# Channel mixer in two groups of six blocks, and plain fp32 scores, in an attention and mixer kernel on one core

## The chip, the cores and the metric

The program runs on one core of one Trainium2 chip, in one launch. The metric is device time in microseconds (us), the median of three runs. A core has a matrix engine (PE, with its weight loads shown as PEld), a vector engine (DVE), an activation engine (ACT), a general engine (POOL), and queues that start DMAs; here all DMAs start from SP's queue (SPq).

## The reference

Four batches of 576 rows. Per batch: eight heads of attention that keep the 32 largest scores of each row, then a gated mixer, then a token mixer and a channel mixer.

```
scores = q @ k.T / 8;  keep the 32 largest of each row;  attn = softmax;  x = attn @ v     # 8 heads of 64
gate = sigmoid(5-tap causal convolution of x);   x = (gate * (x @ w_val)) @ w_out          # 512 x 512 weights
u = x + token mixer(x)                                                                      # 576 -> 256 -> 576
out = u + relu(u @ w_ch1) @ w_ch2                                                           # 512 -> 1536 -> 512
```

The last line is the channel mixer; its 1536 middle features are 12 blocks of 128 rows.

## The kernel before, in words

**Tiling.** Heads are taken in pairs: 16 pairs `p`, batch b = p // 4. A pair has five units: four of 128 query rows for both heads (tile 0 and 1 of a unit, L314 on), one with the last 64 rows of both. For each unit `attn` makes the scores in PSUM in two halves of 288 keys (`Sp`; in batch 0 also the two `mo` tiles), copies them to `S` (L339), folds and finds the 32 largest on DVE (L431, L444 to L446, L461, L463), masks (L374 on ACT, L376 on POOL), takes the exponential (L379), transposes on PE (L388) and multiplies by v (L401 to L405).

**Scores.** The constant `SPLIT = 1, 2, 3` names the batches whose scores are made from two rounded parts. For these `load_pair` splits the loaded `qk` into `qkh` and `qkl` (one ACT copy, L480, and one POOL subtraction, L481, for q and for k of each pair), and a half is six matmuls (`qk3`, L324): high by high, low by high, high by low, each for two heads that stand in rows 0 to 63 and 64 to 127 of the array. In batch 0 a half is two matmuls on the unsplit fp32 data (`qk`, L330), which the trace shows as four, two passes for each head. The last unit of a pair uses plain data in every batch (L348, L350).

**Mixers.** All other large products go through `mm3` (L543 to L545): for each term three matmuls on split operands, 288 columns each. The channel mixer in `mix` runs `G = 3` groups. A group makes four blocks of middle features (weights `ch1`; each block is 2 halves x 4 terms x 3 = 24 matmuls into one `mo` tile), rounds each into a high part (ACT, L487) and a low part (in batches 1 to 3 DVE, L496) in `rh[0..3]`, `rl[0..3]`, then four output tiles (weights `ch2`, 24 matmuls each), each added on to `f` by DVE (`plus`, L652). There are two `mo` tiles.

**Weights.** A weight piece is a `ring` slot (four slots of 128 x 2 x 512). The first time, in batch 0, `piece` loads the 64-bit source, turns it to fp32 on DVE (L515, L519), splits it (ACT, POOL) and stores it in device memory (`ch1d`, `ch2d`); the later batches load it back (L554).

**What sets the order.** `Order` collects all operations with a cost, their dependences and a priority, runs a list schedule for several rounds, and issues the operations in the order of the planned starts. Each engine then works its own queue in that order. So an edit can change the place of any instruction of any engine.

Of the kernel before, what the change touches and what calls it, by code (L numbers as in the profile page):

```python
# [15 lines left out]
NP = B * H // 2  # L16
NEG = -3.0e38
BIG = 2.0 ** 100
G = 3
LO = 1, 2, 3  # L20
CONV = 0,
XOFF = (7, 0, 0, 0)
ROUNDS = 4
PIECES = dict(val=4, out=4, ch1=12, ch2=12)
OFF = -2
WTOK = 24
SPLIT = 1, 2, 3
MOFF = (8, 0, -4, 0)
WOFF = 9

# [136 lines left out]
class Builder:  # L167
    def __init__(self, ctx, tc, qk, v, w_val, conv, w_out, w_tok1, w_tok2, w_ch1, w_ch2, out):
        self.tc, self.nc = tc, tc.nc
        self.qk, self.v, self.out, self.conv = qk, v, out, conv  # L170
        self.wsrc = dict(val=w_val, out=w_out, tok1=w_tok1, tok2=w_tok2, ch1=w_ch1, ch2=w_ch2)
        self.sb = ctx.enter_context(tc.tile_pool(name="sb", bufs=1))
        self.dr = ctx.enter_context(tc.tile_pool(name="dr", bufs=1, space=bass.MemoryType.DRAM))
        self.ps = ctx.enter_context(tc.tile_pool(name="ps", bufs=1, space=bass.MemoryType.PSUM))
        self.o = Order()
        T = self.T
        self.nS, self.nE, self.nW, self.nP = 4, 2, 2, 2
        self.stage = [T(f"stage{i}", [128, 1024], I32) for i in range(2)]
        self.vt = [T(f"v{i}", [128, 11, 64]) for i in range(2)]
        self.qk2 = [T(f"qk{i}", [128, 2, S]) for i in range(2)]  # L180
        self.qkp = [[T(f"qk{x}{i}", [128, 2, S], F32R) for x in "hl"] for i in range(2)]
        self.St = [T(f"S{i}", [128, 2, S]) for i in range(self.nS)]
        self.yt = T("y", [128, 2, S])
        self.At = T("A", [128, 2, 144])
        self.Xt = [T(f"X{i}", [128, 2, 168]) for i in range(2)]
        self.Zt = [T(f"Z{i}", [128, 2, 168]) for i in range(2)]
        self.top = [T(f"top{i}", [128, 2, 32]) for i in range(3)]
        self.nb = [T(f"nb{i}", [128, 2, 2]) for i in range(3)]
        self.Et = [T(f"E{i}", [128, 2 * S]) for i in range(self.nE)]
        self.Wt = [T(f"W{i}", [128, S]) for i in range(self.nW)]  # L190
        self.pT = [T(f"pT{i}", [128, 640]) for i in range(self.nP)]
        self.bad = T("bad", [128, NP * 5, 2, 3])
        self.cst, self.flag, self.worst = T("cst", [1, 1]), T("flag", [1, 1], I32), T("worst", [128, 1])
        self.den = [T(f"den{i}", [128, 4, 9]) for i in range(2)]
        self.rcp = T("rcp", [128, 4, 9])
        self.rhl = T("rhl", [128, 4, 64], F32R)
        self.rT = [T(f"rT{i}", [128, 128], F32R) for i in range(2)]
        self.sel = T("sel", [128, 768], F32R)
        self.ident = T("ident", [128, 128])
        self.diag = T("diag", [128, 5, 128])  # L200
        self.wv = {}
        for n, shp in (("tok1", [128, 2, 5, 256]), ("tok2", [128, 2, 2, S])):
            self.wv[n] = T("w" + n, shp, F32R)
        self.wa = [T(f"wa{i}", [128, S]) for i in range(2)]
        self.made = set()
        self.cw = T("cw", [128, 20])
        self.wd = {n: [self.dr.tile([128, 2, 512], F32, name=f"{n}d{i}") for i in range(k)]
                   for n, k in PIECES.items()}
        self.rs = [T(f"r{i}", [128, S], F32R) for i in range(16)]
        self.fs = [T(f"f{i}", [128, S]) for i in range(4)]  # L210
        self.tf = [T(f"t{i}", [128, S]) for i in range(2)]
        self.xf = [T(f"xf{i}", [128, 4 + S]) for i in range(4)]
        self.nring = 4
        self.ring = [T(f"ring{i}", [128, 2, 512]) for i in range(self.nring)]
        self.Sp = self.ps.tile([128, 2, 512], F32, name="Sp")
        self.PT = self.ps.tile([128, 1024], F32, name="PT")
        self.mo = [self.ps.tile([128, 2, 512], F32, name=f"mo{i}") for i in range(2)]
        self.cnt = dict(mo=0, tf=0, ring=0, rT=0, st=0, wa=0, unit=0, tile=0, load=0)
        self.slot = {}
# [64 lines left out]
    def load_pair(self, p):  # L284

        nc = self.nc
        b, c = divmod(p, 4)
        g = self.slot[p] = self.cnt["load"] % 2
        self.cnt["load"] += 1
        qk = self.qk2[g]  # L290
        for x in (1, 0):
            self.dma(2.3, lambda x=x: nc.sync.dma_start(qk[:, x], self.qk[b, c, :, x]), [], [("qk", g, x)])
        vt = self.vt[g]
        self.dma(2.5, lambda: nc.sync.dma_start(vt, self.v[p]), [], [("v", g)])
        if b in SPLIT and self.fast:
            hi, lo = self.qkp[g]
            for x in (1, 0):
                self.split(qk[:, x], hi[:, x], lo[:, x], [("qk", g, x)], [("qkh", g, x)], [("qkl", g, x)])

    def attn(self, p, u):  # L300

# [8 lines left out]
        R = [("qk", s, 0), ("qk", s, 1)]  # L310

        Sp, kSp = ((self.Sp, "Sp"), (self.mo[0], ("mo", 0)), (self.mo[1], ("mo", 1)))[i % 3 if b == 0 else 0]
        P = self.qkp[s]
        m, kM = self.top[i % 3], [("m", i % 3, t) for t in range(w)]  # L314
        if u < 4:

            for n in range(2):
                c0 = 288 * n

                def qk3(c0=c0):  # L320
                    for x, y in ((0, 0), (0, 1), (1, 0)):
                        for t in range(2):
                            r = slice(64 * t, 64 * t + 64)
                            nc.tensor.matmul(Sp[:, t, 0:288], P[x][r, 0, 128 * u:128 * u + 128],  # L324
                                             P[y][r, 1, c0:c0 + 288], start=(x + y == 0), stop=(x == 1))

                def qk(c0=c0):
                    for t in range(2):
                        r = slice(64 * t, 64 * t + 64)
                        nc.tensor.matmul(Sp[:, t, 0:288], q[r, 128 * u:128 * u + 128], k[r, c0:c0 + 288],  # L330
                                         start=True, stop=True)

                if b in SPLIT and self.fast:
                    self.pe(0.594, qk3, [(z, s, x) for z in ("qkh", "qkl") for x in range(2)], [kSp])
                else:
                    self.pe(0.686, qk, R, [kSp])
                if n and self.fast:
                    self.fold(i, w, St, (Sp[:, :, 0:288], Sp[:, :, 288:432]), kS, kSp)
                self.act(S, lambda c0=c0: nc.scalar.activation(St[:, :, c0:c0 + 288], Sp[:, :, 0:288], AF.Copy),  # L339
                         [kSp], [(x, n) for x in kS] + [kSp] * n)  # L340
# [207 lines left out]
    def piece(self, n, f):  # L548

        nc = self.nc  # L550
        w, k = self.nxt("ring", self.ring)
        kw = [(k, 0), (k, 1)]
        if (n, f) in self.made:
            self.dma(4, lambda: nc.sync.dma_start(w, self.wd[n][f]), [(n, f)], kw)  # L554
        else:
            self.made.add((n, f))
            prio = self.prio
# [1 line left out]
            d = self.dp, self.dd, self.da, self.dl  # L559
            self.dp = self.dd = self.da = self.dl = 0  # L560
            a, ka = self.nxt("wa", self.wa)
            self.f64(self.wsrc[n][f], a[:, 0:512], 128, ka)
            self.split(a[:, 0:512], w[:, 0].bitcast(F32R), w[:, 1].bitcast(F32R), [ka], kw[0:1], kw[1:])
            self.dma(4, lambda: nc.sync.dma_start(self.wd[n][f], w), kw, [(n, f)])
            self.prio = prio
            self.dp, self.dd, self.da, self.dl = d
        return w.bitcast(F32R).rearrange("p a (c f) -> p a c f", c=4), kw

    def gate(self, b, p0):
        nc = self.nc  # L570
# [83 lines left out]
    def mix(self, b):  # L654
# [42 lines left out]
        for c in range(4):  # L697
# [5 lines left out]
                                          for j in range(2)], km, 288)  # L703
            self.plus(x2[c], m, km, K("f", c))
            self.split(x2[c], uh[c], ul[c], K("f", c), K("r", c), K("r", c + 4))
        rh, rl = rs[8:12], rs[12:16]
        for g in range(G):
            for f in range(4):
                self.prio = p0 + 14 + 8 * g + f
                w, kw = self.piece("ch1", g * 4 + f)  # L710
                m, km = self.nxt("mo", self.mo)
                for n, s in halves():
                    self.mm3(m[:, n, 0:288], [(w[:, 0, kc], w[:, 1, kc], uh[kc][:, s], ul[kc][:, s],
                                               K("r", kc, kc + 4) + kw) for kc in range(4)], km, 288)
                self.parts(m[:, :, 0:288], S, two(rh[f]), two(rl[f]), True, b in LO,
                           [km], K("r", 8 + f), K("r", 12 + f))
            for c in range(4):
                self.prio = p0 + 16 + 8 * g + c
                w, kw = self.piece("ch2", g * 4 + c)
                m, km = self.nxt("mo", self.mo)  # L720
                for n, s in halves():
                    self.mm3(m[:, n, 0:288], [(w[:, 0, f], w[:, 1, f], rh[f][:, s], rl[f][:, s],
                                               K("r", 8 + f, 12 + f) + kw) for f in range(4)], km, 288)
                self.plus(fs[c], m, km, K("f", c))
                if g == G - 1:
                    self.dma(2.3, lambda c=c: nc.sync.dma_start(self.out[b, c], fs[c]), K("f", c), [("o", b, c)])
# [95 lines left out]
```

## Time and profile before

| | |
|---|---|
| median of 3 runs | 931.23 us (930.27 to 932.81) |
| profiled execution | 930.93 us, of which the span of instructions is 929.0 us |
| PE busy | 849.0 us (91%) |
| DVE busy | 763.4 us (82%) |
| ACT, POOL busy | 580.2 us (62%), 416.2 us (45%) |
| mean granted PE clock | 0.957 |

The span is what lies between the first and the last instruction; 1.9 us lie around it. A busy share of PE counts a pipelined matmul from its start to its modelled end, so what a matmul costs in a stream is read from the distance between starts. Attention ends at about 792 us; what follows is the last batch's gate, token mixer and channel mixer.

### The profile page before, as it was taken

The numbers are of one execution on the slowest core, as the hardware profiler recorded it, in microseconds if no ns is written. First come the engines' busy times: TensorE is split into PE (matmuls) and PEld (weight loads), VectorE is DVE, ScalarE is ACT, GpSimd is POOL, SyncE is SP. The second block draws the span as 40 slices with busy tenths as digits, with TensorE's granted clock in tenths as the row PEclk, the third lists the DMA queues.
The fourth block names the chain that finished last, engine by engine and source line by source line (L and its number), as shares of the span: only waits on it lengthen the run. The fifth ranks groups of instructions, "written<-read, shape, count | busy, mean of one in ns | idle before, by whom it ended". The sixth has DMA issues, their size and how long they took to land.

```text
span 929.0 us, 18621 instructions
## 1 busy us (share of the span) xinstructions
PE 849.0 (91%) x6649; PEld 731.1 (79%) x6649; DVE 763.4 (82%) x2653; ACT 580.2 (62%) x1279; POOL 416.2 (45%) x377
## 2 busy tenths in 40 slices
PE   4767758999999999999999999999999999889997
PEld 2444446798889987788888889888889999778997
DVE  8999999888999999996799999896997884812221
ACT  4767777857695867757677766676775754422000
POOL 2434555766785867653444433552542312502000
PEclk8878685999999999999999999999999999999999
DMA  3111022455145554623033334333033235222442
GB/s 117 38 47 39 30 67 90 176 180 186 41 162 199 184 186 158 219 92 117 17 121 106 114 108 152 123 117 108 29 105 114 92 106 195 92 92 75 169 164 103
DMA packets 33734, 107.48 MB, mean 116 GB/s; under 512 B 3872, under 2 KB 4128, under 8 KB 33632
## 3 DMA queue, kind: packets, MB, share of 16 engines
q1 hardware_dynamic: 33632, 106.20, 34.1%
q8 instruction: 54, 0.88, 0.4%
q14 instruction: 48, 0.39, 0.1%
HBM read 84.69 MB, written 21.50 MB: 114 GB/s over the span
## 4 chain that ended last, share of the span: by engine, by line
PE 57%; DVE 9%; ACT 6%; POOL 2%; issue 1%; DMA 1%; POOLq 0%; DVEq 0%; ACTq 0%; SPq 0%
PE mo L543 14%; PE mo L544 13%; PE mo L545 13%; PE PT L388 4%; PE Sp L324 4%; PE PT L401 4%; DVE f L630 2%; PE PT L405 2%; ACT r L487 1%; ACT E L379 1%; DVE top L461 1%; DVE Z L463 1%; PE Sp L348 1%; POOL E L376 1%; POOL r L481 1%
## 5 line engine op out<-in xcount | busy, mean ns | idle before, releaser
L543 PE MATMUL mo<-r,ring 128*128 128x288 f32 x1024 | 316.7, 309 | 2.1 <-DVE f L640 1.2
L544 PE MATMUL mo<-r,ring 128*128 128x288 f32 x1024 | 302.7, 296 | 3.0 <-POOL r L481 2.2
L545 PE MATMUL mo<-r,ring 128*128 128x288 f32 x1024 | 301.7, 295 | 0.2 <-POOL ring L481 0.2
L376 POOL TENSOR_TENSOR E<-S,W 128x576 f32<-128x576 f32 x144 | 209.9, 1474 | 89.0 <-ACT W L374 86.5
L543 PEld LDWEIGHTS mo<-r,ring 128*128 128x128 f32 x1024 | 192.3, 188 | 13.0 <-issue 7.8
L544 PEld LDWEIGHTS mo<-r,ring 128*128 128x128 f32 x1024 | 192.5, 188 | 5.3 <-POOL r L481 3.4
L545 PEld LDWEIGHTS mo<-r,ring 128*128 128x128 f32 x1024 | 192.2, 188 | 0.5 <-POOL ring L481 0.5
L388 PE MATMUL PT<-ident,E 128*128 128x128 f32 x656 | 106.7, 294 | 25.3 <-ACT E L379 13.5
L379 ACT ACTIVATE E<-E,nb 128x576 f32<-128x576 f32 x144 | 111.5, 775 | 25.4 <-POOL E L376 24.2
L461 DVE MAX8 top<-Z 128x8 f32<-128x168 f32 x432 | 126.1, 325 | 0.5
L393 ACT ACTIVATE pT<-PT 128x512 f32<-128x512 f32 (+1 forms) x144 | 94.3, 655 | 47.8 <-PE PT L388 47.2
L388 PEld LDWEIGHTS PT<-ident,E 128*128 128x128 f32 x656 | 79.4, 149 | 42.9 <-ACT pT L393 18.6
L374 ACT ACTIVATE W<-S,nb 128x576 f32<-128x576 f32 x144 | 106.1, 771 | 0.2
L487 ACT ACTIVATE r<-mo 128x576 fp32r<-128x576 f32 (+2 forms) x76 | 46.9, 632 | 85.8 <-PE mo L545 80.4
L401 PE MATMUL PT<-pT,v 128*64 128x128 f32 (+1 forms) x640 | 88.5, 286 | 12.0 <-ACT pT L393 11.3
L450 POOL TENSOR_TENSOR bad<-X,top 128x6 f32<-128x6 f32 (+1 forms) x80 | 23.1, 289 | 165.6 <-DVE top L461 153.7
L401 PEld LDWEIGHTS PT<-pT,v 128*64 128x64 f32 x640 | 69.4, 147 | 30.2 <-ACT pT L393 19.7
L652 DVE TENSOR_TENSOR f<-mo,f 128x576 f32<-128x576 f32 x64 | 48.0, 751 | 53.2 <-PE mo L545 53.0
L463 DVE MATCH_REPLACE8 Z<-top,Z 128x168 f32<-128x168 f32 x288 | 90.1, 319 | 0.0
L402 PE MATMUL PT<-pT,v 128*64 128x128 f32 (+1 forms) x640 | 88.5, 286 | 0.0
L339 ACT ACTIVATE S<-Sp 128x576 f32<-128x576 f32 x108 | 69.8, 647 | 26.6 <-DVE y L431 12.4
L481 POOL TENSOR_TENSOR r<-f,r 128x576 fp32r<-128x576 f32 x32 | 48.2, 1512 | 62.1 <-ACT r L480 62.0
(124 smaller groups left out, 1679.2 us busy)
## 6 DMA issues: line engine op xcount, KB each, us to landing
ring<-ch1d SPq DMA_DIRECT2D x36, 512.0 KB, 3.3
ring<-ch2d SPq DMA_DIRECT2D x36, 512.0 KB, 3.2
stage<-in_w_ch_dram SPq DMA_DIRECT2D x24, 512.0 KB, 3.6
qk<-in_qk_dram SPq DMA_DIRECT2D x32, 288.0 KB, 3.2
ch1d<-ring SPq DMA_DIRECT2D x12, 512.0 KB, 5.1
ch2d<-ring SPq DMA_DIRECT2D x12, 512.0 KB, 2.6
ring<-vald SPq DMA_DIRECT2D x12, 512.0 KB, 3.9
ring<-outd SPq DMA_DIRECT2D x12, 512.0 KB, 3.2
```

What stands on the lines that cost most here:

```text
L374: self.act(S, lambda W=W, x=x, t=t: nc.scalar.activation(W, x, AF.Relu, bias=nb[:, t, 1:2], scale=-BIG), kx + [(kN, 1)], [kW], True)
L376: self.pool(S, lambda W=W, x=x, E=E: nc.gpsimd.tensor_tensor(E, x, W, op=OP.subtract), kx + [kW], [kE])
L379: self.act(S + 110, lambda E=E, d=d, t=t: nc.scalar.activation(E, E, AF.Exp, bias=nb[:, t, 0:1], scale=0.125, accum_out=d), [kE, (kN, 0)], ...
L388: nc.tensor.transpose(self.PT[:, y * 128:(y + 1) * 128], E2[:, k * 128:(k + 1) * 128], self.ident)
L393: self.act(n, lambda pT=pT, n=n: nc.scalar.activation(pT[:, 0:n], self.PT[:, 0:n], AF.Copy), kp, [kP])
L401: nc.tensor.matmul(o[0:64, 0:n], vt[:, y], a[:, y * 128:y * 128 + n], start=(y == 0), stop=False)
L402: nc.tensor.matmul(o[64:128, 0:n], vt[:, 6 + y], e[:, y * 128 + g:y * 128 + 128], start=(y == 0), stop=False)
L461: self.dve(n, lambda src=src, o=o: v.max(o, src), k, [(kM, q)] + [kM] * (q in (0, 3)))
L463: self.repl(n, lambda src=src, o=o: v.match_replace(out=z, in_to_replace=o, in_values=src, imm_value=NEG), k + [(kM, q)], [kz])
L543: nc.tensor.matmul(o, wh, xh, start=(x == 0), stop=False)
L544: nc.tensor.matmul(o, wh, xl, start=False, stop=False)
L545: nc.tensor.matmul(o, wl, xh, start=False, stop=(x == last))
```

## The change

Two edits. The channel mixer takes two groups of six blocks, and the `ch2` weights come in 16 pieces of 3 x 128 rows where they were 12 of 4 x 128, so that an output tile of a group needs two pieces (and two ring slots) and is 36 matmuls. `rh` and `rl` grow to six tiles each. Scores are plain fp32 in all batches: `qk3`, the split tiles and their ACT and POOL operations go.

```diff
-G = 3
+G, GF = 2, 6
+KC = dict(val=4, out=4, ch1=4, ch2=3)
-PIECES = dict(val=4, out=4, ch1=12, ch2=12)
+PIECES = dict(val=4, out=4, ch1=12, ch2=16)
-SPLIT = 1, 2, 3
@@ load_pair
-        if b in SPLIT and self.fast:
-            hi, lo = self.qkp[g]
-            for x in (1, 0):
-                self.split(qk[:, x], hi[:, x], lo[:, x], [("qk", g, x)], [("qkh", g, x)], [("qkl", g, x)])
@@ attn
-                if b in SPLIT and self.fast:
-                    self.pe(0.594, qk3, [(z, s, x) for z in ("qkh", "qkl") for x in range(2)], [kSp])
-                else:
-                    self.pe(0.686, qk, R, [kSp])
+                self.pe(0.686, qk, R, [kSp])
@@ piece
         w, k = self.nxt("ring", self.ring)
+        w = w[:, :, 0:128 * KC[n]]
@@ mix
-        rh, rl = rs[8:12], rs[12:16]
+        rh, rl = rs[8:8 + GF], rs[8 + GF:8 + 2 * GF]
         for g in range(G):
-            for f in range(4):
-                self.prio = p0 + 14 + 8 * g + f
-                w, kw = self.piece("ch1", g * 4 + f)
+            for f in range(GF):
+                self.prio = p0 + 14 + 12 * g + f
+                w, kw = self.piece("ch1", g * GF + f)
...
             for c in range(4):
-                self.prio = p0 + 16 + 8 * g + c
-                w, kw = self.piece("ch2", g * 4 + c)
+                self.prio = p0 + 18 + 12 * g + c
                 m, km = self.nxt("mo", self.mo)
+                ws = [self.piece("ch2", (2 * g + x) * 4 + c) for x in range(2)]
                 for n, s in halves():
-                    self.mm3(m[:, n, 0:288], [(w[:, 0, f], w[:, 1, f], rh[f][:, s], rl[f][:, s],
-                                               K("r", 8 + f, 12 + f) + kw) for f in range(4)], km, 288)
+                    self.mm3(m[:, n, 0:288], [(w[:, 0, f], w[:, 1, f], rh[3 * x + f][:, s], rl[3 * x + f][:, s],
+                                               K("r", 8 + 3 * x + f, 8 + GF + 3 * x + f) + kw)
+                                              for x, (w, kw) in enumerate(ws) for f in range(3)], km, 288)
                 self.plus(fs[c], m, km, K("f", c))
```

Line numbers of the changed kernel are about 14 to 16 lower: L324 and L330 become L317, L543 to L545 become L527 to L529.

How the order changes at three places. First, PE at a score half of batch 1 while the mixers of batch 0 run (before; `qkh_69` and `qkl_70` are the split parts, `mo_177` the tile that a mixer product fills):

```order
L543 MATMUL mo_177<-r_146,ring_174 128x288
L544 MATMUL mo_177<-r_150,ring_174 128x288
L545 MATMUL mo_177<-r_146,ring_174 128x288
L324 MATMUL Sp<-qkh_69 128x288 x2
L324 MATMUL Sp<-qkl_70,qkh_69 128x288 x2
L324 MATMUL Sp<-qkh_69,qkl_70 128x288 x2
L543 MATMUL mo_177<-r_147,ring_174 128x288
L544 MATMUL mo_177<-r_151,ring_174 128x288
L545 MATMUL mo_177<-r_147,ring_174 128x288
```

The same kind of place in the changed kernel, a score half of batch 1 between two terms of batch 0's token mixer:

```order
L527 MATMUL mo_181<-r_147,wtok_104 128x512
L528 MATMUL mo_181<-r_152,wtok_104 128x512
L529 MATMUL mo_181<-r_147,wtok_104 128x512
L317 MATMUL Sp<-qk_68 128x288 x2
L527 MATMUL mo_181<-r_148,wtok_104 128x512
L528 MATMUL mo_181<-r_153,wtok_104 128x512
L529 MATMUL mo_181<-r_148,wtok_104 128x512
```

The half stands alone between mixer matmuls as before, with two written matmuls instead of six. Second, PE in the last batch at the first output tile of a channel mixer group (before; `r_153` to `r_156` are the high parts of the four blocks, `r_157` to `r_160` the low parts):

```order
L543 MATMUL mo_177<-r_153,ring_171 128x288
L544 MATMUL mo_177<-r_157,ring_171 128x288
L545 MATMUL mo_177<-r_153,ring_171 128x288
L543 MATMUL mo_177<-r_154,ring_171 128x288
L544 MATMUL mo_177<-r_158,ring_171 128x288
L545 MATMUL mo_177<-r_154,ring_171 128x288
L543 MATMUL mo_177<-r_155,ring_171 128x288
L544 MATMUL mo_177<-r_159,ring_171 128x288
L545 MATMUL mo_177<-r_155,ring_171 128x288
L543 MATMUL mo_177<-r_156,ring_171 128x288
L544 MATMUL mo_177<-r_160,ring_171 128x288
```

In the changed kernel the same tile, from the third of its six terms on (`r_153` to `r_158` high, `r_159` to `r_164` low):

```order
L527 MATMUL mo_181<-r_155,ring_177 128x288
L528 MATMUL mo_181<-r_161,ring_177 128x288
L529 MATMUL mo_181<-r_155,ring_177 128x288
L527 MATMUL mo_181<-r_156,ring_178 128x288
L528 MATMUL mo_181<-r_162,ring_178 128x288
L529 MATMUL mo_181<-r_156,ring_178 128x288
L527 MATMUL mo_181<-r_157,ring_178 128x288
L528 MATMUL mo_181<-r_163,ring_178 128x288
L529 MATMUL mo_181<-r_157,ring_178 128x288
L527 MATMUL mo_181<-r_158,ring_178 128x288
L528 MATMUL mo_181<-r_164,ring_178 128x288
```

The newest block's low part is read 11 matmuls into the tile before, and 17 matmuls into it now. Third, SP's queue of weight loads in a later batch, before:

```order
L554 DMA ring_174<-ch1d_124 128x1024
L554 DMA ring_171<-ch2d_133 128x1024
L554 DMA ring_172<-ch2d_134 128x1024
L554 DMA ring_173<-ch2d_135 128x1024
L554 DMA ring_174<-ch2d_136 128x1024
L554 DMA ring_171<-ch1d_125 128x1024
```

and now:

```order
L539 DMA ring_176<-ch1d_122 128x1024
L539 DMA ring_177<-ch2d_129 128x2x384
L539 DMA ring_178<-ch2d_133 128x2x384
L539 DMA ring_175<-ch2d_130 128x2x384
L539 DMA ring_176<-ch2d_134 128x2x384
L539 DMA ring_177<-ch2d_131 128x2x384
L539 DMA ring_178<-ch2d_135 128x2x384
```

Four loads per group of output tiles became eight smaller ones, two per tile, in the same four slots.

## Rows read from the trace of the kernel before

**Rows 1.** Page: span; busy us, share, instructions of an engine.

```profile
span 929.0 us, 18621 instructions
PE 849.0 (91%) x6649; PEld 731.1 (79%) x6649; DVE 763.4 (82%) x2653; ACT 580.2 (62%) x1279; POOL 416.2 (45%) x377
```

**Rows 2.** Stretches: us, busy of PE, PEld, DVE, ACT, POOL; clock; DMA share, GB/s.

```profile
0.00:164.00 164.00, 113.36 (x719) 74.97 (x721) 159.45 (x657) 116.53 (x272) 71.92 (x79) 0.77 0.19 61
164.00:440.00 276.00, 264.62 (x2119) 231.03 (x2116) 257.81 (x836) 200.80 (x443) 188.27 (x153) 0.99 0.47 160
440.00:787.00 347.00, 343.10 (x2889) 304.44 (x2887) 298.21 (x1101) 233.40 (x519) 137.02 (x134) 1.00 0.32 106
787.00:929.00 142.00, 127.96 (x930) 120.69 (x929) 47.97 (x60) 29.45 (x49) 18.96 (x12) 0.99 0.35 117
...
114.00:124.00 10.00, 6.29 (x50) 3.96 (x50) 9.97 (x48) 7.95 (x21) 4.63 (x6) 1.00 0.00 0
```

**Rows 3.** PE's waits from 164 to 787 us: total us, times, longest.

```profile
PE PT L388 <- ACT pT L393: 2.7, 4, 1.2
PE PT L401 <- ACT pT L393: 2.7, 5, 0.9
```

**Rows 4.** PE timeline, a split score half: start, us, line, tiles, xcount.

```profile
240.52 0.29 PE L545 MATMUL mo<-wtok,r 128*128 128x288 f32 x1
240.74 0.41 PE L324 MATMUL Sp<-qkh 64*128 64x288 f32 x2
240.98 0.30 PE L324 MATMUL Sp<-qkl,qkh 64*128 64x288 f32 x2
241.12 0.30 PE L324 MATMUL Sp<-qkh,qkl 64*128 64x288 f32 x2
241.34 0.27 PE L401 MATMUL PT<-pT,v 128*64 128x64 f32 x1
```

**Rows 5.** PE timeline, two plain score halves of batch 0, one behind the other.

```profile
118.14 0.51 PE L330 MATMUL mo<-qk 64*128 64x288 f32 x2
...
118.48 0.41 PE L330 MATMUL mo<-qk 64*128 64x288 f32 x2
118.73 0.65 PE L330 MATMUL Sp<-qk 64*128 64x288 f32 x4
119.31 0.32 PE L401 MATMUL PT<-pT,v 128*64 128x128 f32 x1
```

**Rows 6.** Operations by tile: ns min/median/max, first and last start us, forms.

```profile
L324 PE MATMUL Sp<-qkh x192: 290/397/607, 143.3 to 756.0; 64*128 64x288 f32 x192
L480 ACT ACTIVATE qkh<-qk x24: 667/683/708, 97.8 to 677.8; 128x576 fp32r<-128x576 f32 x24
L481 POOL TENSOR_TENSOR qkl<-qk,qkh x24: 1402/1426/1617, 100.3 to 678.6; 128x576 fp32r<-128x576 f32 x24
L652 DVE TENSOR_TENSOR f<-mo,f x64: 734/757/759, 244.5 to 922.8; 128x576 f32<-128x576 f32 x64
```

**Rows 7.** Timeline, last batch, first output tile of a group, and PE's wait of that kind from 787 us on.

```profile
857.85 0.65 ACT L487 ACTIVATE r<-mo 128x576 fp32r<-128x576 f32 x1 [2.53 <-PE mo L545]
...
858.53 0.76 DVE L496 SCALAR_TENSOR_TENSOR r<-mo,r 128x576 fp32r<-128x576 f32 x1 [2.43 <-ACT r L487]
...
858.85 0.29 PE L543 MATMUL mo<-r,ring 128*128 128x288 f32 x1
859.35 0.40 PE L544 MATMUL mo<-r,ring 128*128 128x288 f32 x1 [0.21 <-DVE r L496]
...
PE mo L544 <- DVE r L496: 0.6, 3, 0.2
```

**Rows 8.** Page: DMA issues of the weight pieces: count, KB each, median us to landing.

```profile
ring<-ch1d SPq DMA_DIRECT2D x36, 512.0 KB, 3.3
ring<-ch2d SPq DMA_DIRECT2D x36, 512.0 KB, 3.2
```

**Rows 9.** Groups by line: busy us, mean ns, idle before: splits of weight pieces on POOL and ACT.

```profile
L481 POOL TENSOR_TENSOR ring<-wa,ring 128x512 fp32r<-128x512 f32 x32 | 41.4, 1296 | 32.7 <-ACT ring L480 20.7 <-issue 11.1 <-POOL bad L450 0.8
```

More of the change, by code (lines that the diff above doesn't have):

```diff
@@ L180, in __init__ @@
         self.qk2 = [T(f"qk{i}", [128, 2, S]) for i in range(2)]
-        self.qkp = [[T(f"qk{x}{i}", [128, 2, S], F32R) for x in "hl"] for i in range(2)]
         self.St = [T(f"S{i}", [128, 2, S]) for i in range(self.nS)]
@@ L206, in __init__ @@
         self.cw = T("cw", [128, 20])
-        self.wd = {n: [self.dr.tile([128, 2, 512], F32, name=f"{n}d{i}") for i in range(k)]
+        self.wd = {n: [self.dr.tile([128, 2, 128 * KC[n]], F32, name=f"{n}d{i}") for i in range(k)]
                    for n, k in PIECES.items()}
-        self.rs = [T(f"r{i}", [128, S], F32R) for i in range(16)]
+        self.rs = [T(f"r{i}", [128, S], F32R) for i in range(8 + 2 * GF)]
         self.fs = [T(f"f{i}", [128, S]) for i in range(4)]
@@ L312, in attn @@
         Sp, kSp = ((self.Sp, "Sp"), (self.mo[0], ("mo", 0)), (self.mo[1], ("mo", 1)))[i % 3 if b == 0 else 0]
-        P = self.qkp[s]
         m, kM = self.top[i % 3], [("m", i % 3, t) for t in range(w)]
@@ L318, in attn @@
                 c0 = 288 * n
[L320 to L325, printed above, removed]
                 def qk(c0=c0):
@@ L551, in piece @@
         w, k = self.nxt("ring", self.ring)
+        w = w[:, :, 0:128 * KC[n]]
         kw = [(k, 0), (k, 1)]
         if (n, f) in self.made:
-            self.dma(4, lambda: nc.sync.dma_start(w, self.wd[n][f]), [(n, f)], kw)
+            self.dma(KC[n], lambda: nc.sync.dma_start(w, self.wd[n][f]), [(n, f)], kw)
         else:
@@ L561, in piece @@
             a, ka = self.nxt("wa", self.wa)
-            self.f64(self.wsrc[n][f], a[:, 0:512], 128, ka)
-            self.split(a[:, 0:512], w[:, 0].bitcast(F32R), w[:, 1].bitcast(F32R), [ka], kw[0:1], kw[1:])
-            self.dma(4, lambda: nc.sync.dma_start(self.wd[n][f], w), kw, [(n, f)])
+            self.f64(self.wsrc[n][f], a[:, 0:w.shape[2]], 128, ka)
+            self.split(a[:, 0:w.shape[2]], w[:, 0].bitcast(F32R), w[:, 1].bitcast(F32R), [ka], kw[0:1], kw[1:])
+            self.dma(KC[n], lambda: nc.sync.dma_start(self.wd[n][f], w), kw, [(n, f)])
             self.prio = prio
             self.dp, self.dd, self.da, self.dl = d
-        return w.bitcast(F32R).rearrange("p a (c f) -> p a c f", c=4), kw
+        return w.bitcast(F32R).rearrange("p a (c f) -> p a c f", f=128), kw
     def gate(self, b, p0):
@@ L715, in mix @@
                 self.parts(m[:, :, 0:288], S, two(rh[f]), two(rl[f]), True, b in LO,
-                           [km], K("r", 8 + f), K("r", 12 + f))
+                           [km], K("r", 8 + f), K("r", 8 + GF + f))
             for c in range(4):
-                self.prio = p0 + 16 + 8 * g + c
-                w, kw = self.piece("ch2", g * 4 + c)
+                self.prio = p0 + 18 + 12 * g + c
                 m, km = self.nxt("mo", self.mo)
+                ws = [self.piece("ch2", (2 * g + x) * 4 + c) for x in range(2)]
                 for n, s in halves():
-                    self.mm3(m[:, n, 0:288], [(w[:, 0, f], w[:, 1, f], rh[f][:, s], rl[f][:, s],
-                                               K("r", 8 + f, 12 + f) + kw) for f in range(4)], km, 288)
+                    self.mm3(m[:, n, 0:288], [(w[:, 0, f], w[:, 1, f], rh[3 * x + f][:, s], rl[3 * x + f][:, s],
+                                               K("r", 8 + 3 * x + f, 8 + GF + 3 * x + f) + kw)
+                                              for x, (w, kw) in enumerate(ws) for f in range(3)], km, 288)
                 self.plus(fs[c], m, km, K("f", c))
@@ L806 @@
         'w_ch1': blocks(inputs['moe2_w_ch1']),
-        'w_ch2': np.reshape(np.transpose(np.reshape(inputs['moe2_w_ch2'], (3, 4, 128, 4, 128)), (0, 3, 2, 1, 4)),
-                            (12, 128, 512)),
+        'w_ch2': np.reshape(np.transpose(np.reshape(inputs['moe2_w_ch2'], (4, 3, 128, 4, 128)), (0, 3, 2, 1, 4)),
+                            (16, 128, 384)),
     }
```

## The prediction

> **What bounds the kernel now.** I read the busy shares first, then the stretches, then PE's waits, then PE's timeline at single places. The page says that PE is busy 91% of the span and DVE 82% [rows 1]; the stretches say where. Up to 164 us DVE sets the pace: it is busy 159.5 of 164.0 us while PE is busy 113.4 at a mean granted clock of 0.77 [rows 2]. From 164 to 440 us PE is busy 264.6 of 276.0 us and idle 11.4; from 440 to 787 us it is busy 343.1 of 347.0 and idle 3.9, at full clock [rows 2]. So for 623 us PE has 15.3 us of idle time, and its work bounds the program. DVE is close behind it in the first of these stretches (257.8 of 276.0 us). What PE does wait for is late work of the attention chain: the copies of transposed tiles on ACT lead the list [rows 3]. From 787 us on only the last batch's mixers are left, PE is idle 14.0 us of 142.0 [rows 2], and waits there are latencies between dependent steps. The reader is to take from this: work added to PE behind 164 us is paid almost in full, work taken from DVE, ACT or POOL pays only through PE's 15.3 us of waits.
>
> **The change part by part.** *Plain scores.* A half of split scores starts at 240.74 us and the next PE instruction at 241.34: 0.60 us [rows 4]. Inside it a pass over 288 columns (both heads side by side) takes 0.14 us from start to start, and the entry and the exit, where the shape of the operands in the array changes, take some 0.1 us each (0.24 us to the second pass, 0.22 us behind the last). There are 192 such matmuls of the first kind, two for each half, so 96 halves, from 143.3 to 756.0 us [rows 6]: all but a few lie where PE bounds.
>
> A plain half is seen only in batch 0. I take the two at 118.14 us, where the clock is 1.00 [rows 2, 5]. The first pass takes 0.34 us to the next start at 118.48, the second 0.25 us; both halves together, one behind the other, take 119.31 - 118.14 = 1.17 us [rows 5]. Taking the third pass as 0.25 as well, the last one with its exit is 1.17 - 0.34 - 0.25 - 0.25 = 0.33 us. A half that stands alone between other work pays entry and exit: 0.34 + 0.33 = 0.67 to 0.69 us with the rounding. In batches 1 to 3 there is one `Sp` tile, a second half must wait for ACT's copy of the first, and the order puts other work between them, so the halves do stand alone, as the split ones do. The difference is 0.07 to 0.10 us; I take 0.09 us. 96 x 0.09 = **8.6 us more on PE**. From above 96 x 0.10 = 9.6. From below, if all halves cost what two in a row cost on average (0.585 us), 96 x -0.015 = -1.4 us.
>
> The trace shows the plain half as two passes of 0.25 us where the split one has three of 0.14 [rows 4, 5]. The Trainium skill (FP8 and Floating Point Precision, TensorE Precision Notes) says that a true fp32 product takes four passes through the array, each high or low part by each. Four passes in place of three at 0.14 us would make it 96 x 0.14 = 13.4 us instead of 8.6, and the time 940.8 (an estimate by that rule). The trace agrees on the count, since 0.25 us is two passes of 0.125, and differs on the size, since these passes are each a little shorter than the split ones; the measured rows decide for the sum.
>
> *Splits of q and k that go.* 24 ACT copies of 0.683 us are 16.4 us, 24 POOL subtractions of 1.426 us are 34.2 us [rows 6]. Neither engine bounds a stretch [rows 2], so nothing of this is on the path by itself; it counts as earlier releases, below. Batch 0's first 97 us have no such split [rows 6], so the DVE bound head keeps its length.
>
> *Two groups of six.* The number of matmuls is the same: 3 x 4 x 24 = 288 for `ch2` before, 2 x 4 x 36 = 288 now, and `ch1` has the same twelve tiles. DVE's additions go from 12 to 8 per batch: 16 x 0.757 = 12.1 us of DVE over the kernel [rows 6], 3.0 of it in the last batch, where DVE is busy only 48.0 of 142.0 us [rows 2]. In the last batch a real wait goes. Before, the first output tile of a group reads the newest block's low part as its 11th matmul; ACT and DVE make that part in series (857.85 to 859.29 us), and PE stands from 858.85 to 859.35, 0.50 us instead of 0.13 [rows 7]. There are three such waits [rows 7], 3 x 0.37 = 1.1 us. Now the part is read at the 17th matmul, 6 x 0.13 = 0.8 us later, more than the wait. **1.1 us less**; nothing is late behind it, since the tile's weights are there long before. If another part were late instead, 0.
>
> *Weight pieces.* The bytes are the same. Each output tile takes 36 x 0.133 = 4.8 us and two of the four slots. Its first piece is last read in matmul 27 of 36 and its slot is next needed two tiles on: 9 + 36 matmuls, 6.0 us; the second likewise, 36 + 9. A 512 KB piece lands 3.2 us after its issue [rows 8], and a piece now has 384 KB, so the transfer is covered by 2.8 us; four more issues per batch stand in SP's queue in the same order. I take 0. If landing doubled, some 0.4 us for each of 32 tiles, 12 us, would show. In batch 0 the pieces are converted: as many columns in 16 operations instead of 12. The POOL split is 1.30 us for 512 columns [rows 9]; if the shorter ones cost as much, 4 x 1.30 = 5.2 us of POOL, in a stretch in which POOL is busy 188.3 of 276.0 us [rows 2]. DVE's conversions grow likewise by 12 short operations, less than the additions that go. I take 0.
>
> *Earlier releases.* PE's 15.3 us of waits between 164 and 787 us can shrink: ACT loses 16.4 of 434 us there (4%), POOL 34.2 of 325 (11%), DVE 9.1 of 556 (2%). In proportion this is 17% of 15.3 us: **2.5 us less**. From both sides: 0, or all 15.3.
>
> Sum on the profiled execution: 930.9 + 8.6 - 1.1 - 2.5 = 935.9 us. It lies 0.3 us below the median of the runs, so 936 us.
>
> **The rivals.** *No change, the wait takes up the price.* If the planner fills PE's idle time with the added work, 7.5 us of the 15.3 go in place of 2.5: 930.9 + 8.6 - 1.1 - 7.5 = 931 us. For it speaks that two thirds of the idle time lie in one stretch in which DVE is 93% busy, which the change relieves; against it, that the waits are for ACT's copies, which the change leaves as they are.
>
> *Faster: the stretch from 164 to 440 us is paced by DVE and POOL, and PE only follows.* Then relief there pays at once and all 11.4 us of PE's idle time goes: 930.9 + 8.6 - 1.1 - 11.4 = 927 us. It decides once PE's idle time in this stretch falls below 2 us. Against it: PE is already at 96% there, and DVE loses only some 5 us in it.
>
> *Slower by more: two slots per tile starve batch 0's mixer.* Where pieces are still converted, an output tile waits for two conversions, and the POOL split of the second (1.30 us, rows 9) is exposed once for each of batch 0's 8 tiles: 10.4 us more, 930.9 + 8.6 - 1.1 - 2.5 + 10.4 = 946 us. For it: POOL's and ACT's queues are long there. Against it: the other work of batch 1's attention fills PE while it waits.
>
> **How the numbers follow.** Forecast 0.55, with its own range 933 to 939 (the pass price from 0.07 to 0.10 us, the releases from 0 to 5 us). No change 0.20, faster 0.10, starved 0.10, the four-pass price 0.05. A measurement of this kernel tells 0.3% (2.8 us) from no change, so faster is below 928.4 and slower above 934.0. Slower: 0.50 of the forecast's 0.55, 0.10 and 0.05, together 0.65. Same: 0.05 of the forecast and 0.18 of the no-change case, 0.23. Faster: 0.10 and 0.02, 0.12. The range goes from 928.5 to 941: it leaves out most of the faster case and most of the starved one.
>
> **What would show it.** Right: a lone plain half of 0.67 to 0.69 us at full clock, PE busy longer by about 8 us between 164 us and the end of attention, no wait at the first output tile of a group in the last batch, PE idle time of 12 to 13 us in the middle. Wrong: plain halves of under 0.62 us, PE idle below 8 us in the middle, PE waits for `ring` in batch 0 or for a DMA in the last batch, or a head that ends at another time than 164 us, since DVE's part of it was taken as unchanged.

## The result and the profile after

The changed kernel takes 938.93 us (median of 7 runs, 937.24 to 942.78), the kernel before in the same comparison 932.38 us (7 runs, 928.27 to 935.2). The ratio is 1.008, with a 95% interval of 1.0053 to 1.0107: 7.5 us more, between 4.9 and 10.0. The forecast was 936.0 us, 5.1 more than its profiled execution, and slower at 0.65. The direction and the range held; as a difference, 7.5 us stand against 5.1. The experiments say which step was short, and where two of the terms did not do what was said of them.

The profiled execution of the changed kernel took 942.78 us, the longest of the seven, so it must not be read as typical in every place. Its page, against [rows 1]:

```profile
span 941.0 us, 18204 instructions
PE 867.0 (92%) x6457; PEld 727.3 (77%) x6457; DVE 753.9 (80%) x2649; ACT 571.3 (61%) x1259; POOL 382.3 (41%) x357
```

PE is busy 18.0 us longer and idle 6.0 us less (74.0 us instead of 80.0): together the span's 12.0 us. DVE, ACT and POOL all work less. So the loss is on PE. The smaller idle time does not yet show relief by the other engines: a second run of the kernel before, with nothing changed, is idle 74.3 us, because a lower clock makes PE's work longer (below). The stretches, with the columns of [rows 2], say where:

```profile
0.00:164.00 164.00, 116.34 (x696) 74.92 (x697) 160.75 (x659) 115.14 (x269) 68.43 (x77) 0.74 0.21 70
164.00:440.00 276.00, 268.21 (x2011) 228.46 (x2010) 243.16 (x795) 191.46 (x421) 168.25 (x142) 0.96 0.45 152
440.00:787.00 347.00, 344.03 (x2752) 292.82 (x2751) 303.59 (x1138) 234.15 (x519) 126.44 (x127) 1.00 0.32 100
787.00:941.00 154.00, 138.41 (x1005) 131.12 (x1003) 46.37 (x59) 30.55 (x52) 19.18 (x12) 0.98 0.40 126
```

PE's idle time from 164 to 787 us is 7.8 + 3.0 = 10.8 us, where it was 15.3. Taken to the end of attention, which comes later now, it is 11.9 us. Note the granted clock of the second stretch: 0.96, where it was 0.99. Clock was withheld there; this comes back below.

The new score half, to be held against [rows 4], stands alone between two mixer matmuls (start, busy us, line, tiles):

```profile
543.05 0.29 PE L529 MATMUL mo<-r,ring 128*128 128x288 f32 x1
543.26 0.76 PE L317 MATMUL Sp<-qk 64*128 64x288 f32 x4
543.95 0.40 PE L527 MATMUL mo<-r,ring 128*128 128x288 f32 x1
```

From 543.26 to 543.95 are 0.69 us, where the split half took 0.60. All score halves together, on their one line (the columns PE and PEld, then the stretch's clock, DMA share and GB/s; first before, then the changed kernel):

```profile
440.00:787.00 347.00, 37.22 (x336) 24.14 (x336) 1.00 0.32 106
sum 623.00, PE 62.47 PEld 40.49; mean PE 31.23 PEld 20.25
```

```profile
440.00:787.00 347.00, 42.35 (x224) 16.88 (x224) 1.00 0.32 100
sum 623.00, PE 72.72 PEld 29.27; mean PE 36.36 PEld 14.64
```

From 164 to 787 us that is 10.2 us more. A part of it is the lower clock of this execution: in the stretch at full clock 56 halves (224 instructions, four each) take 5.13 us more, 0.09 each, and with the order of before the sum is 8.7 us, as the first experiment shows.

At the first output tile of a group in the last batch, the place of [rows 7], the changed kernel shows this:

```profile
875.85 0.65 ACT L471 ACTIVATE r<-mo 128x576 fp32r<-128x576 f32 x1 [2.53 <-PE mo L529]
...
876.54 0.76 DVE L480 SCALAR_TENSOR_TENSOR r<-mo,r 128x576 fp32r<-128x576 f32 x1 [2.42 <-ACT r L471]
...
878.05 0.29 PE L527 MATMUL mo<-r,ring 128*128 128x288 f32 x1
878.18 0.29 PE L528 MATMUL mo<-r,ring 128*128 128x288 f32 x1
878.31 0.30 PE L529 MATMUL mo<-r,ring 128*128 128x288 f32 x1
```

The newest block's low part is ready at 877.30 us, and the matmul that reads it (878.18) follows its predecessor after 0.13 us: the wait is gone. What the groups are worth in the last batch can be read between its first and its last mixer addition on DVE (ns min/median/max, first and last start in us; before, then now):

```profile
L652 DVE TENSOR_TENSOR f<-mo,f x16: 757/758/758, 839.4 to 922.8; 128x576 f32<-128x576 f32 x16
```

```profile
L637 DVE TENSOR_TENSOR f<-mo,f x12: 756/757/759, 851.1 to 933.1; 128x576 f32<-128x576 f32 x12
```

83.4 us became 82.0, so 1.4 us are gained there. All five traces of kernels with three groups have 83.4 or 83.5 us and all four with two groups 82.0 or 82.1.

In this trace PE waits for no weight piece; in the other traces with two groups it does a little (below). The pieces land as soon as before [rows 8], at 3.4 us for 384 KB instead of 3.2 for 512:

```profile
ring<-ch1d SPq DMA_DIRECT2D x36, 512.0 KB, 3.3
ring<-ch2d SPq DMA_DIRECT2D x48, 384.0 KB, 3.4
```

### The profile page after: what moved, and what is told of

Read it like the earlier page. It is cut to its first block, busy times and chain, and to the rows that moved or that the text cites. A ratio compares the mean times of both kernels' runs of the same rounds, so it can differ in the third digit from the quotient of the medians.

```text
span 941.0 us, 18204 instructions
## 1 busy us (share of the span) xinstructions
PE 867.0 (92%) x6457; PEld 727.3 (77%) x6457; DVE 753.9 (80%) x2649; ACT 571.3 (61%) x1259; POOL 382.3 (41%) x357
## 4 chain that ended last, share of the span: by engine, by line
PE 69%; DVE 22%; ACT 4%; DMA 1%; POOL 1%; issue 1%; POOLq 0%; SPq 0%; DVEq 0%; ACTq 0%
PE mo L527 15%; PE mo L528 14%; PE mo L529 14%; PE Sp L317 6%; PE PT L372 6%; PE PT L385 5%; DVE top L445 4%; DVE Z L447 4%; DVE wa L503 3%; DVE y L415 2%; PE mo L607 2%; PE PT L389 2%; DVE X L428 2%; PE Sp L332 1%; DMA stage<-in_w_ch_dram 1%
## 5 line engine op out<-in xcount | busy, mean ns | idle before, releaser
L527 PE MATMUL mo<-r,ring 128*128 128x288 f32 x1024 | 318.4, 311 | 4.2 <-DVE f L625 3.3
L529 PE MATMUL mo<-r,ring 128*128 128x288 f32 x1024 | 303.0, 296 | 0.0
L360 POOL TENSOR_TENSOR E<-S,W 128x576 f32<-128x576 f32 x144 | 206.3, 1448 | 98.2 <-ACT W L358 94.8
L527 PEld LDWEIGHTS mo<-r,ring 128*128 128x128 f32 x1024 | 193.6, 189 | 24.6 <-issue 17.3
L529 PEld LDWEIGHTS mo<-r,ring 128*128 128x128 f32 x1024 | 193.5, 189 | 0.0
L372 PE MATMUL PT<-ident,E 128*128 128x128 f32 x656 | 110.8, 302 | 21.7 <-ACT E L363 14.7
L372 PEld LDWEIGHTS PT<-ident,E 128*128 128x128 f32 x656 | 82.0, 153 | 45.6 <-ACT E L363 20.2
L317 PE MATMUL Sp<-qk 64*128 64x288 f32 x432 | 89.6, 491 | 10.6 <-ACT S L323 5.7
L637 DVE TENSOR_TENSOR f<-mo,f 128x576 f32<-128x576 f32 x48 | 36.1, 752 | 58.0 <-PE mo L529 57.6
```

Source lines behind the costliest of these rows:

```text
L360: self.pool(S, lambda W=W, x=x, E=E: nc.gpsimd.tensor_tensor(E, x, W, op=OP.subtract), kx + [kW], [kE])
L372: nc.tensor.transpose(self.PT[:, y * 128:(y + 1) * 128], E2[:, k * 128:(k + 1) * 128], self.ident)
L527: nc.tensor.matmul(o, wh, xh, start=(x == 0), stop=False)
L529: nc.tensor.matmul(o, wl, xh, start=False, stop=(x == last))
```

## Experiments

Theory: the price is the plain half's extra time on PE, some 8.6 us, paid in full; the loss of the split operations and the new groups give some of it back. Main rival: PE's waits absorb the price, and the loss comes from the new groups or from the changed order. Seven runs were made, in two sets on two chips, each compared with the kernel before on the same chip; the last three runs form the second set.

**The price alone, order kept.** The written matmuls become plain, while the splits are still made and the planner is told the same costs and, beside the plain data, the same reads as before. The traces have the same order on every engine. The split parts are computed and not used.

```diff
-  self.pe(0.594, qk3, [(z, s, x) for z in ("qkh", "qkl") for x in range(2)], [kSp])
+  self.pe(0.594, qk, [(z, s, x) for z in ("qkh", "qkl") for x in range(2)] + R, [kSp])
```

> The kernel before with plain fp32 matmuls in the score halves of batches 1 to 3, and everything else kept: the splits of q and k are still made (unused by the halves), the planned cost is left at 0.594, so every engine's order is that of before. Theory (a lone plain half costs PE 0.09 us more): 96 x 0.09 = 8.6 us slower than before, 938 to 941 us, PE busy between 164 and 790 us up by about 8 us, granted clock as before. Rival (four passes at the split price, 0.14 us each): 12 to 14 us slower. Rival (the price of a half is small and the change was slow because the planner put the work in another order): within 3 us of before.

Measured: 940.39 us, ratio 1.0085 (1.0056 to 1.0115), 7.9 us more (5.2 to 10.7). The score halves from 164 to 787 us, with the columns as above:

```profile
164.00:440.00 276.00, 28.89 (x148) 11.64 (x148) 0.99 0.48 160
440.00:787.00 347.00, 42.31 (x224) 16.86 (x224) 1.00 0.31 100
sum 623.00, PE 71.20 PEld 28.50; mean PE 35.60 PEld 14.25
```

At the clock of before (0.99 and 1.00) the halves take 71.20 - 62.47 = 8.7 us more, and the time rises by 7.9. The price is of the size worked out, and with the order kept the waits of PE absorb none of it that can be told.

**A fourth product.** The other direction: split scores as before, with low times low added as a fourth product (more work than the reference needs), and the planned cost left alone.

```diff
-  for x, y in ((0, 0), (0, 1), (1, 0)):
+  for x, y in ((0, 0), (0, 1), (1, 1), (1, 0)):
...
-  start=(x + y == 0), stop=(x == 1))
+  start=(x + y == 0), stop=(x > y))
```

> The kernel before with a fourth split product (low by low) in each score half of batches 1 to 3, planned cost left at 0.594, order of before on every engine. It measures how fully PE time added at these places is paid. Theory (PE bounds, next to nothing is absorbed): 96 x 0.13 = 12.5 us slower than before. Rival (PE's waits absorb added work): less than 8 us slower.

Measured: 944.29 us, ratio 1.0141 (1.0114 to 1.0168), 13.2 us more (10.6 to 15.7). The score halves:

```profile
164.00:440.00 276.00, 29.32 (x288) 20.70 (x288) 1.00 0.47 158
440.00:787.00 347.00, 44.50 (x448) 31.50 (x448) 1.00 0.32 101
sum 623.00, PE 73.82 PEld 52.20; mean PE 36.91 PEld 26.10
```

Busy time grows by 11.4 us from 164 to 787 us, and 96 x 0.13 us (one pass, as the mixer's passes start) would be 12.5. Again nothing is absorbed. The two runs give a line: 8.7 us of work on PE cost 7.9 us, 11.4 us cost 13.2, both within their intervals of one to one.

**Plain scores, splits gone.** The scores' half of the change alone: the 24 ACT copies and 24 POOL subtractions go too, and the planner orders anew.

```diff
-SPLIT = 1, 2, 3
+SPLIT = ()
```

> The kernel before with SPLIT empty: plain scores in all batches, the splits of q and k gone, three groups of four kept, order planned anew. Theory: 8.6 us more on PE less 2 us of earlier releases, 6 to 7 us slower than before. Rival (the two groups of six are what costs): within 2 us of before. Rival (the lower granted clock in the middle comes with plain scores): a stretch of half clock between 300 and 450 us and a time above 940 us.

Measured: 936.5 us, ratio 1.0045 (1.0019 to 1.0072), 4.2 us more (1.8 to 6.7). Against the price alone it is 3.7 us better by the ratios, 3.9 by the medians, 2.7 by the mean spans (-0.1 to 5.5, so not clear of noise by these alone). The forecast was 2.5. The rival that all of the price is absorbed falls. But the place where the gain was to come from does not show it: PE's idle time from 164 us to the end of attention is 16.3 us in this trace, 14.8 with the price alone and 15.3 and 15.4 in the two traces of the kernel before. It falls only when the groups change too, to 11.9 and 12.5 us in the two traces of the changed order. So what the missing splits give back, and by which wait, stays open. The rival that plain scores bring half clock in the middle and more than 940 us is not borne out as a rule: the profiled execution, at 943.5 us, has half clock from 386 to 393 us, but the median is 936.5.

**Groups of six alone.** The changed kernel with the split scores of batches 1 to 3 put back.

```diff
 G, GF = 2, 6
+SPLIT = 1, 2, 3
@@ load_pair
+        if b in SPLIT and self.fast:
+            hi, lo = self.qkp[g]
+            for x in (1, 0):
+                self.split(qk[:, x], hi[:, x], lo[:, x], ...)
@@ attn
-                self.pe(0.686, qk, R, [kSp])
+                if b in SPLIT and self.fast:
+                    self.pe(0.594, qk3, ..., [kSp])
+                else:
+                    self.pe(0.686, qk, R, [kSp])
```

> The changed kernel with split scores in batches 1 to 3 put back: two groups of six alone, order planned anew. Theory: the three waits at the first output tile of a group in the last batch go (1.1 us) and 12 us of DVE additions go where DVE does not bound: 0 to 3 us faster than before, no wait of PE for a weight piece. Rival (two ring slots per output tile starve PE): slower than before by 3 us or more, with PE waits for ring.

Measured: 938.06 us, ratio 1.0076 (1.0047 to 1.0106), 7.1 us more (4.4 to 9.9). This is the miss: by the forecast the groups give 1.1 us back. They do so in the last batch of this kernel too, as the additions show. The loss lies elsewhere. This trace and the first trace of the kernel before have the same clock over the first 170 us (0.78), so they can be laid side by side behind it; there two traces of one kernel agree within a microsecond, as the last run below shows. Attention ends 3.0 us later (795.7 us instead of 792.7): PE is idle 0.8 us and busy 2.2 us longer from 164 us on. The last mixer's first addition comes another 2.2 us later, where the clock falls in this trace and does not in the other, and 1.4 us come back behind it. The last 1.6 us are at the end.

A part of the 3.0 us is the rival of the two slots: PE waits 1.3 us for the split of a weight piece on POOL, in batch 0, where it waited 0.2 us before. In columns of total us, times and longest, first before, then here:

```profile
PE mo L545 <- POOL ring L481: 0.2, 1, 0.2
```

```profile
PE mo L546 <- POOL ring L482: 1.3, 3, 0.6
```

Two marks of this trace were followed further. The first stands at the end. SP's last semaphore operations (columns: count, ns, first and last start in us), before and in this kernel:

```profile
L817 SPq EVENT_SEMAPHORE  x10: 17/28/28, 927.7 to 929.0; - x10
```

```profile
L820 SPq EVENT_SEMAPHORE  x10: 17/28/28, 931.7 to 934.5; - x10
```

The row of ten takes 1.3 us before and 2.8 us here, so SP stands inside it: for 1.5 us, from 931.8 us on. The pages' rows of DMA queues differ by one instruction transfer (packets, MB, share), before and here:

```profile
q14 instruction: 48, 0.39, 0.1%
```

```profile
q14 instruction: 49, 0.40, 0.2%
```

The changed kernel has both marks: 49 transfers, and a last row of 2.8 us (938.1 to 940.9). A load of code at the end was the theory for 1.5 us, and the next two kernels test it. The second mark is the granted clock, below.

**The end's code moved.** The program has a second part that is jumped over in these runs. 24 more loads in that part shift the code behind it, change nothing that is executed, and so move the place at which the end has to be fetched. Two kernels: the groups alone, and the whole change. Their diffs are the same line:

```diff
-  self.dma(2.5, lambda: nc.sync.dma_start(vt, self.v[p]), [], [("v", g)])
+  [self.dma(2.5, lambda: nc.sync.dma_start(vt, self.v[p]), [], [("v", g)]) for _ in range(1 if self.fast or p else 25)]
```

> Two groups of six with split scores as in the run with groups only, and 24 more loads of v in the second part of the program, which is jumped over in every execution: the part that runs keeps its order on every engine. In the runs with two groups SP stands 1.5 us inside its last row of waits, 7.1 us from the last addition to the end instead of 5.4. Theory (it is a load of code: the last instructions of SP lie across a border of the loaded pieces, and the number of SP instructions sets where it lies): with the border moved the end is 5.4 us again, and the time 1.5 us below the run with groups only. Rival (SP waits for a late store of the output): the end stays at 7.1 us.

> The changed kernel with the same 24 loads more in the part that is jumped over. Theory: end of 5.4 us instead of 7.1, time 1.5 us below the changed kernel, about 937.5 us; and a second trace of the changed kernel's order. If the stretch of half clock from 386 to 406 us belongs to the order, it is here again; if it belongs to the single execution, it is not.

Measured: the groups alone 936.71 us, ratio 1.0031 (1.0006 to 1.0056), 2.9 us more than before (0.6 to 5.2); the whole change 937.36 us, ratio 1.0063 (1.0028 to 1.0097), 5.9 us more (2.6 to 9.0). The last semaphore row of the first and of the second, which takes 1.3 us again in each:

```profile
L820 SPq EVENT_SEMAPHORE  x10: 17/28/28, 934.6 to 935.9; - x10
```

```profile
L803 SPq EVENT_SEMAPHORE  x10: 17/28/28, 930.1 to 931.4; - x10
```

Both pages count 48 instruction transfers. So 1.5 us of the change's loss is a stop at the very end that goes when code that is never executed is moved; it does not come from the program's work. That SP waits there for a load of code is what fits the count, though no row names it as the releaser: in the two traces with the stop the additional transfer starts behind it, not in it. The timed runs agree in size: the mean span falls by 2.6 us (0.2 to 4.9, between the two chips) and by 2.0 us (-0.9 to 4.9, so not shown by that pair alone). Both stay slower than before, so the stop is not the whole of the miss. Waits for weights are small here too: PE waits 0.9 us for a split on POOL in the first of these traces and 0.5 us for a piece's transfer in the second.

**The kernel before once more.** Unchanged, one run, to see how far two executions of one program differ.

> The kernel before, unchanged, for a second trace. If the granted clock behind 170 us is set by the order, there is again one stretch of half clock of 3.4 us, near 227 us; if it differs from execution to execution, there are others, and the time differs by half their length.

Measured: 935.78 us, a single run, with a span of 934.0 us where the first trace of the same program has 929.0. All of it arises early. Its first 170 us, first in the trace of before, then here (columns of [rows 2]):

```profile
0.00:170.00 170.00, 119.36 (x752) 79.51 (x753) 165.41 (x674) 122.03 (x286) 76.94 (x85) 0.78 0.20 64
```

```profile
0.00:170.00 170.00, 125.39 (x729) 82.37 (x729) 160.35 (x663) 118.34 (x275) 72.25 (x80) 0.69 0.18 59
```

At a clock of 0.69 instead of 0.78, DVE has done 5 us less work by 170 us. The way from the one to the other can be read in the trace. From 110 to 130 us the clock is 0.76, where it was 1.00. PE's last product of a pair (L408) ends later, and SP's queue holds the next load of `v` until then, with everything behind it. So two loads of weight source start 4.3 us later (first before, then here), and DVE, which is to convert them, stands for 3.9 us:

```profile
124.94 0.33 SPq L294 DMA_DIRECT2D v<-in_v_dram  x1
128.31 0.87 SPq L510 DMA_DIRECT2D stage<-in_w_tok_dram  x2
```

```profile
128.43 0.33 SPq L294 DMA_DIRECT2D v<-in_v_dram  x1
132.61 0.85 SPq L510 DMA_DIRECT2D stage<-in_w_tok_dram  x2
137.66 2.97 DVE L515 TENSOR_SCALAR wa<-stage 128x512 int32<-128x512 int32 x2 [3.92 <-DMA stage<-in_w_tok_dram]
```

The trace with plain scores and no splits has the same wait (4.4 us). Batch 0 ends 5 us later (its last addition is at 393 us instead of 388), and from there on both traces run within a microsecond of each other's pace. The stretch of half clock near 227 us is here again, near 232 us. So the head is not paced by DVE alone, and one trace of a kernel stands for its kernel to some 5 us only. Differences of that size between single traces prove nothing here; the comparisons of timed runs do.

**The clock in all runs.** The timed runs of the two sets and of the changed kernel list their span and mean granted clock. Span x (1 - clock) is the time withheld. Over 37 runs of the four kernels with groups of six it is 49.8 us in the mean, over 62 runs of the others 45.9: 3.9 us more (1.5 to 6.3). For the 18 runs with the groups alone it is 2.6 us more than for the kernel before, not clear of nothing (-0.5 to 5.8). Among runs of one and the same kernel, one more microsecond withheld goes with 0.42 us more span (standard error 0.03, all kernels pooled), most of the withheld time being in the head. By that the groups' 3.9 us would be worth 1.6 us (an estimate: no run sets the clock by itself); if all of it is withheld where PE bounds, up to 3.9. At equal withheld time by the same 0.42, the groups alone still take 4.2 us more than the kernel before, and 3.1 with the end's code moved, so the clock is not the whole of it either. The traces show where such a fall lies. Five-microsecond stretches of the changed kernel (columns of [rows 2]):

```profile
380.00:385.00 5.00, 4.96 (x43) 3.52 (x40) 4.96 (x20) 4.47 (x13) 2.53 (x4) 1.00 0.88 283
385.00:390.00 5.00, 3.79 (x15) 3.00 (x15) 4.42 (x10) 4.70 (x12) 2.31 (x3) 0.54 0.12 47
390.00:395.00 5.00, 4.61 (x25) 3.16 (x26) 5.00 (x23) 4.10 (x10) 4.01 (x4) 0.50 0.02 3
395.00:400.00 5.00, 5.00 (x36) 4.09 (x36) 3.13 (x8) 1.20 (x4) 0.62 (x1) 0.50 0.01 2
400.00:405.00 5.00, 5.00 (x21) 4.24 (x22) 4.65 (x8) 3.03 (x8) 1.62 (x2) 0.50 0.26 74
405.00:410.00 5.00, 5.00 (x36) 5.00 (x36) 4.54 (x12) 4.07 (x8) 3.89 (x3) 0.91 0.32 99
```

and the same place in the kernel before:

```profile
380.00:400.00 20.00, 18.27 (x163) 15.55 (x164) 19.71 (x55) 15.18 (x35) 12.06 (x10) 1.00 0.39 132
800.00:840.00 40.00, 35.49 (x232) 31.33 (x231) 15.15 (x21) 11.23 (x18) 6.52 (x4) 1.00 0.31 106
```

Where batch 0 ends, the changed kernel's PE runs at the lower level (1.2 GHz) for some 20 us; in the five microseconds in which the clock falls PE is busy 3.79 us, in those before it 4.96. The whole change with its end's code moved has the same order and falls there for about 7 us only, so an order does not fix the length. The groups alone fall there too (0.91 from 380 to 400 us), and in the last batch (0.94 from 800 to 840 us). But the plain scores without new groups fall there as well (0.83 and 0.96), so falls are not peculiar to the groups; only their mean share is. Why the clock falls at these places was not tested.

## Why the prediction came out as it did

**The price of plain scores (8.6 us): right.** Lone half 0.69 us as forecast, 8.7 us more busy time and 7.9 us more time (5.2 to 10.7) with the order kept. The sign of about 8 us more busy time of PE up to the end of attention came out as 8.8 us with the price alone, and as 14.1 and 7.0 us in the two traces of the changed order, whose clocks differ. The lower bound, two halves one behind the other, never came into play. On the rule of four passes for a true fp32 product (the Trainium skill, FP8 and Floating Point Precision, TensorE Precision Notes): at split passes' length it would have made 13.4 us, and the runs decide against that size, since four written split products add 11.4 us of busy time and the plain product 8.7. On the count of passes the rows decide nothing: 0.25 us from start to start [rows 5] has room for two, and no row shows one by itself.

**Earlier releases (2.5 us): the size fits, the mechanism is half shown.** The step from the price alone to splits gone gives 3.7 us, with an interval that reaches down to nothing. The sign that was named, 12 to 13 us of PE idle time in the middle, is there for the whole change: 11.9 and 12.5 us to the end of attention. It is not there for plain scores alone (16.3), nor for the groups alone (16.1 and 17.3). Adding up the shares by which three engines are relieved had no ground in a wait, so that the size fits is in part luck.

**Two groups of six (1.1 us less): the step that failed.** The prediction counted the three waits of the last batch and "nothing is late behind it". The waits went, as [rows 7] let one work out, and the last batch's mixer is 1.4 us shorter. But the sum put everything else that the new order does at nothing. Measured, the groups alone cost 7.1 us (4.4 to 9.9), and with the end's code moved 2.9 (0.6 to 5.2). What the runs put in place of the term: 1.5 us at the end, shown by the two kernels with moved code; some 3 us before the end of attention in that kernel's trace, of which PE's waits for split weight pieces are 1.1 us and the rest is not traced to a cause; and clock withheld, worth 1.6 us by the slope over all timed runs and up to 3.9, which is an estimate and in part the same time. Inside the change the same step is smaller: the changed kernel lies 2.4 us above plain scores alone by the medians (938.93 and 936.5), 3.3 by the ratios, and -1.1 + 1.5 + 1.6 = 2.0 is of that size without being shown to be its cause.

**The sum.** 8.6 - 1.1 - 2.5 = 5.0 was forecast. With 8.7 for the price, 3.7 given back and 2.0 for the groups, it is 7.0, against the measured 7.5 (4.9 to 10.0); only the first of these three is firm. That the forecast was only 2.9 us off owes something to luck: costs of the new order and of the end were missing, and the gain that was counted seems to be too small by about a microsecond.

**Weight pieces (0): right within a microsecond.** The trace of the changed kernel has no wait of PE for a slot or a transfer, the second trace of its order 0.5 us for a transfer, and the groups alone 1.3 and 0.9 us for splits of pieces in batch 0. The rival of starved slots named this mechanism; its size, 10.4 us and a time of 946 us, is false.

**The rivals of no change and of faster: false.** For the first, 7.5 us of PE's waits had to go; about 3 went. For the second, the idle time from 164 to 440 us had to fall below 2 us; it is 7.8 even with DVE relieved by 14.7 us there, so PE does not merely follow DVE.

**The head (same length): not shown.** It was said to keep its length because DVE bounds it. The repeated run of the kernel before shows the head 5 us longer at a lower clock with no change at all, by the way of a late `v` load and the weight loads behind it, so that sign could not have told anything.

## What to carry to other kernels

Work on the bounding engine can be priced from one lone instance between its real neighbours, times its count: entry and exit included, this gave the busy time to 0.1 us, and the time within its interval. Relief of engines that don't bound pays little; here 50.6 us of ACT and POOL work removed gave some 3.7 us, and not where it was expected. A new order can cost something by itself: a gain read at one place holds for that place alone. Before a term of 1 or 2 us is trusted, look at what the order doesn't show, the end of the program and the granted clock of each stretch, and at how far two traces of one program differ.

## What was not expected of the hardware

- Ten semaphore operations at the end take 1.3 us, or 2.8 us when SP stops among them for 1.5 us; the runs with that stop have one more instruction transfer (49 instead of 48 on the instruction queue). Code that is never executed decides which.
- One program, traced twice, spans 929.0 and 934.0 us, with a granted clock of 0.78 and 0.69 over its first 170 us. The slower PE reached DVE through a queue: 4.3 us of delay of two weight loads became 3.9 us of DVE standing.
- One order of instructions had the clock at half for some 20 us near 390 us in one execution, and for some 7 us in another. PE had been busy 4.96 of the five microseconds before the longer fall.
